# K and Q made ahead, values in three widths, and spaced reuse of two shared PSUM banks in a one-core attention kernel

## The chip, the cores and the metric

The kernel runs on one core of one Trainium2 chip. The metric is the device time of one execution in microseconds (us). The mean granted TensorE clock of each run is given too. The 21 executions of the kernel before that stood beside the experiments lie up to 1.7% to either side of their mean, so a timed experiment has four executions, with executions of the kernel before on the same chip beside it.

## The reference

```python
# x: [2048, 640] bf16, H = 32 heads of 20 columns
g = sigmoid((x * gate_w).sum(-1, keepdims=True))
q, k, v = split_heads(x @ wqkv)
a = concat_heads(softmax(q @ k.T * 20**-0.5) @ v) @ wo
h = x @ w1 + b1                     # [2048, 1536]
b = (h * tanh(softplus(h))) @ w2    # Mish
out = g * a + (1 - g) * b
```

Softmax dominates: 32 heads with 2048 x 2048 scores each. The kernel cuts them into 2048 blocks of 128 keys by 512 queries. A *group* is one chunk of 512 queries and four heads: 64 blocks, 32 groups in all, numbered 0 to 31. Groups 0 to 7 are the first query chunk.

## The kernel before

Scores come out of TensorE into PSUM, ScalarE applies the exponential to two or three blocks at a time (a *tile*, or *slot*, t), and TensorE multiplies the result by the values into `acc`. To relieve ScalarE, some pairs of blocks go to VectorE, which makes the exponential by integer arithmetic. Such a block has three terms and needs three value matmuls in place of one.

PSUM has eight banks' worth of tiles here: five for the scores of ScalarE, one for `acc`, and **two shared banks**. The shared banks take everything else: the *units* (projections K, Q, V and later the matrices of the dense branch) and the scores of the VectorE blocks. A unit alternates the banks. A VectorE score takes the bank that the next unit would take:

```python
def next_bank():
    ubank[0] ^= 1
    return banks[ubank[0]][:, :]

DPAIRS0 = (18, 34, 50)       # VectorE pairs in groups 1 to 7, block offsets
DPAIRS = (14, 30, 46, 62)    # in groups 8 to 31
LEAD = 20                    # a VectorE block is scored that many blocks ahead

def emit_D(n):
    ...
    d = banks[ubank[0] ^ 1]          # picked first ...
    scores(d[:, :], blocks[n])       # ... then K and Q are required: may run units here
    nc.vector.tensor_scalar(out=A[:, i, :], in0=d[:, :], ...)     # the eviction dA
```

Units stand in a queue, each with a slot by which it is due. `pump` gives TensorE some columns of them in each slot. If a score needs a K chunk (16 blocks) that isn't there, `require` runs the queue on the spot until it is. The slot loop is, in short:

```python
for t, ns in enumerate(tiles):
    nc.scalar.activation(E, sp.pop(t), ACT.Exp, scale=escale)   # exponential of tile t
    flush_acts()                                                # now and then: Mish
    if t in later: later.pop(t)()       # VectorE parts of a group's normalisation
    emit_S(t + 2)                       # scores two tiles ahead
    if todo and todo[0] - ns[-1] <= LEAD and gap <= 0:
        emit_D(todo.pop(0)); gap = 2
    for fn in dve_q[:2]: fn()           # VectorE exponential, two operations
    ...
    pv_quads(...)                       # value matmuls
    pump(...)                           # units, at most one (group 0: two) finished
```

A TensorE instruction that waits for a bank holds up the scores behind it: in the stretch from 64.79 us on, shown below, TensorE does nothing for 2.25 us while one unit waits for a bank. Four times, once for each query chunk, ScalarE computes Mish and makes no exponential for 8.1 us; these are the *Mish pauses*. The *tail* is what is left after the last group's exponentials.

The softmax here doesn't subtract the row's maximum and nothing guards it: scores larger than these inputs give would overflow.

## Time and profile before

| | before |
|---|---|
| median of the first 3 runs | 1058.92 us (1052.11 to 1073.89) |
| profiled run | span 1064.9 us, mean clock 0.885 |
| TensorE, ScalarE, VectorE busy | 918, 883, 652 us |
| group 0; groups 1-4; 5-7; 8-30; 31 and tail | 55.4; 137.6; 102.2; 717.9; 51.8 us |

The group times are read from the starts of the 31 copies `accS<-acc`, one at the end of each group but the last. From the page of the kernel before, busy times, then the load of TensorE and ScalarE and the granted clock in tenths, in 40 slices of the span:

```profile
PE 917.6 (86%) x6174; PEld 270.6 (25%) x6174; DVE 652.0 (61%) x1260; ACT 882.7 (83%) x750; POOL 19.8 (2%) x36
...
PE   6989888898888969998968898996998896989994
...
ACT  2979887778777899998998999989898888789771
...
PEclk8999997978689889999989999989899877799577
```

Neither TensorE nor ScalarE is full. The clock drops in places, above all in slices 7 to 15 and near the end. The clock is read with the windows view. Here are four neighbouring stretches of 3.41 us, laid on the grid of the clock records (columns: stretch, length, busy time and count of TensorE, weight load, VectorE, ScalarE, Pool; clock; DMA):

```profile
61.37:64.79 3.42, 3.42 (x32) 1.35 (x31) 1.07 (x2) 3.25 (x4) 0.00 (x0) 1.00 0.03 2
64.79:68.20 3.41, 1.16 (x9) 0.59 (x8) 2.99 (x7) 1.76 (x2) 0.00 (x0) 1.00 0.00 0
68.20:71.61 3.41, 3.41 (x22) 1.16 (x19) 2.12 (x6) 1.45 (x1) 0.00 (x0) 0.50 0.03 5
71.61:75.03 3.42, 2.51 (x13) 0.70 (x10) 1.54 (x4) 2.48 (x2) 0.52 (x1) 1.00 0.01 2
```

In the second stretch TensorE is busy for 1.16 us of 3.41; the rest is one wait for a bank. The next stretch runs at half clock: TensorE is then busy all the time, with fewer instructions (22 against 32). So a stall may be paid twice, in itself and in the half clock after it. The waits view names what makes TensorE and ScalarE wait (engine and line, what for, us in total, times, longest):

```profile
ACT E L743 <- PE Sp L565: 124.7, 153, 3.5
PE Sp L565 <- ACT E L743: 46.6, 59, 8.2
PE bank_74 L364 <- DVE dA L588: 9.6, 9, 3.1
PE bank_74 L330 <- DVE dA L588: 9.3, 9, 1.8
PE bank_74 L229 <- DVE dA L588: 8.5, 11, 1.9
PE bank_73 L565 <- DVE kT L238: 4.9, 4, 2.3
PE bank_73 L565 <- DVE hst L338: 3.9, 3, 1.9
```

`bank_73` and `bank_74` are the shared banks. L565 is a score; L229, L330 and L364 are units; L588 is the eviction (the copy out of PSUM) of a VectorE score. `kT`, `qT` and `hst` are the copies of K, Q and `h` that VectorE makes out of a shared bank. All rows of this kind together come to 69 us, 47.6 of it waits for `dA`, all but 0.9 by units. They go before the falls of the clock: of the 19 falls that follow neither the start, nor a Mish pause, nor the very end, 17 come after a piece of 3.4 us in which at least 80% of TensorE's idle time was such waits. The timeline shows how a K chunk that is not there holds up TensorE (start, length, instruction, idle time before it):

```profile
73.34 0.39 PE L229 MATMUL bank_73<-xT,wkp_104 128*128 128x512 bf16 x1
...
73.77 0.69 DVE L238 CAST kT<-bank_73 128x512 bf16<-128x512 f32 x1 [1.40 <-PE bank_73 L229]
...
74.52 0.38 PE L565 MATMUL bank_74<-qT,kT 32*128 32x512 bf16 x1 [0.79 <-DVE kT L238]
...
74.94 0.69 DVE L588 TENSOR_SCALAR dA<-bank_74 128x512 int16<-128x512 f32 x1 [0.48 <-PE bank_74 L565]
75.68 0.67 PE L271 MATMUL bank_74<-W_sb,xT 128*128 128x240 bf16 x5 [0.78 <-DVE dA L588]
```

K is finished just before the score that reads it, the score waits 0.79 us for its copy, and then the next unit, in the same bank as the score, waits 0.78 us for `dA`.

### The profile page before, as it was taken

Reading aid. Unit: us, or ns where it says so; the run is one execution under the profiler, and the core shown is the slowest. Engines: PE = TensorE matmul, PEld = TensorE weight load, DVE = VectorE, ACT = ScalarE, POOL = GpSimd, SP = SyncE. Lnnn points to the kernel's source line nnn. Section 1 sums busy time; section 2 is a strip of 40 time slices with the busy share of each in tenths; the row PEclk is TensorE's granted clock in tenths of the full one; section 3 lists DMA queues with packets and bytes.
Section 4 is the critical chain, followed back from the end, with each engine's and each line's share of the span. In section 5 each row is a group of like instructions: output and inputs, shape, how many; then the busy total and the mean of one; then the engine's idle time right before and its main releaser. Section 6 shows DMA issues by size and latency. Waiting matters only on the chain.

```text
span 1064.9 us, 15307 instructions
## 1 busy us (share of the span) xinstructions
PE 917.6 (86%) x6174; PEld 270.6 (25%) x6174; DVE 652.0 (61%) x1260; ACT 882.7 (83%) x750; POOL 19.8 (2%) x36
## 2 busy tenths in 40 slices
PE   6989888898888969998968898996998896989994
PEld 3433332222122212222212222221232221222221
DVE  2366555545466747776765777766577664577556
ACT  2979887778777899998998999989898888789771
POOL 5000000000000000000000000000000000000000
PEclk8999997978689889999989999989899877799577
DMA  7000000000400000000000000000000000000000
GB/s 226 5 2 1 2 1 1 2 1 1 149 1 2 2 1 1 8 8 14 2 1 2 1 8 14 7 1 2 2 1 2 2 1 1 14 13 1 1 2 25
DMA packets 22215, 14.16 MB, mean 13 GB/s; under 512 B 15968, under 2 KB 20192, under 8 KB 22144
## 3 DMA queue, kind: packets, MB, share of 16 engines
q1 hardware_dynamic: 20512, 12.16, 3.8%
q0 software_dynamic: 320, 0.82, 0.4%
q8 instruction: 48, 0.79, 0.3%
q10 hardware_dynamic: 1312, 0.20, 0.1%
q14 instruction: 23, 0.19, 0.1%
HBM read 10.04 MB, written 2.62 MB: 12 GB/s over the span
## 4 chain that ended last, share of the span: by engine, by line
PE 51%; DVE 21%; ACT 18%; issue 4%; DMA 3%; SPq 2%; DVEq 0%; ACTq 0%
ACT E L743 15%; PE Sp L565 14%; PE acc L637 14%; DVE dA L588 5%; PE bank_74 L364 3%; PE bank_73 L364 3%; PE bank_73 L229 3%; PE bank_74 L229 3%; PE bank_74 L330 2%; PE bank_73 L330 2%; DVE dm L614 2%; PE bank_73 L565 2%; DVE dm L607 2%; ACT hst L352 1%; PE bank_74 L565 1%
## 5 line engine op out<-in xcount | busy, mean ns | idle before, releaser
L743 ACT ACTIVATE E<-Sp 128x1536 bf16<-128x1536 f32 x726 | 847.4, 1245 | 143.5 <-PE Sp L565 124.7
L565 PE MATMUL Sp<-qT,kT 32*128 32x512 bf16 x1814 | 316.5, 416 | 52.4 <-ACT E L743 46.6
L637 PE MATMUL acc<-E,VA 128*32 128x512 bf16 x1814 | 218.7, 426 | 4.9 <-DVE accS L654 4.6
L588 DVE TENSOR_SCALAR dA<-bank_73 128x512 int16<-128x512 f32 x118 | 81.2, 688 | 140.7 <-PE bank_73 L565 129.9
L565 PEld LDWEIGHTS <-kT 32*128 32x128 bf16 x2048 | 82.7, 92 | 294.3 <-issue 263.5
L588 DVE TENSOR_SCALAR dA<-bank_74 128x512 int16<-128x512 f32 x116 | 79.4, 684 | 93.5 <-PE bank_74 L565 89.1
L637 PEld LDWEIGHTS <-VA 128*32 128x32 bf16 x2516 | 70.3, 97 | 190.9 <-issue 178.2
L614 DVE TENSOR_TENSOR dm<-dm 128x1024 f16<-128x1024 f16 x117 | 80.6, 689 | 2.6
L616 DVE TENSOR_TENSOR dB<-dA,dm 128x1024 bf16<-128x1024 bf16 x117 | 79.7, 681 | 0.0
L565 PE MATMUL bank_73<-qT,kT 32*128 32x512 bf16 x118 | 49.4, 419 | 10.4 <-DVE kT L238 4.9
L565 PE MATMUL bank_74<-qT,kT 32*128 32x512 bf16 x116 | 47.4, 409 | 9.5 <-DVE kT L238 3.6
L330 PE MATMUL bank_74<-xT,w_sb 128*128 128x512 bf16 x125 | 45.8, 419 | 9.3 <-DVE dA L588 9.3
L611 DVE TENSOR_SCALAR dm<-dm 128x1024 f16<-128x1024 bf16 x117 | 50.2, 429 | 4.0
L607 DVE TENSOR_SCALAR dm<-dA 128x1024 int16<-128x1024 int16 x117 | 50.0, 427 | 4.0
L637 PE MATMUL acc<-dN,VA 128*32 128x512 bf16 x234 | 51.5, 437 | 0.1
L637 PE MATMUL acc<-dA,VA 128*32 128x512 bf16 x234 | 51.1, 433 | 0.0
L637 PE MATMUL acc<-dB,VA 128*32 128x512 bf16 x234 | 51.0, 433 | 0.0
L364 PE MATMUL bank_74<-w_sb,hst 128*128 128x320 bf16 x192 | 45.9, 323 | 5.9 <-DVE dA L588 4.8
L615 DVE TENSOR_SCALAR dN<-dA 128x1024 int16<-128x1024 int16 x117 | 49.5, 423 | 0.0
L364 PE MATMUL bank_73<-w_sb,hst 128*128 128x320 bf16 x192 | 44.3, 321 | 3.7 <-DVE dA L588 3.6
L364 PEld LDWEIGHTS <-hst 128*128 128x128 bf16 x384 | 26.3, 99 | 69.5 <-issue 65.7
L330 PE MATMUL bank_73<-xT,w_sb 128*128 128x512 bf16 x115 | 40.6, 403 | 2.2 <-DVE dA L588 2.2
(102 smaller groups left out, 617.2 us busy)
## 6 DMA issues: line engine op xcount, KB each, us to landing
w_sb<-in_B_w_dram SPq DMA_DIRECT2D x2, 1920.0 KB, 10.3
x_sb<-in_A_x_dram SPq DMA_DIRECT2D x4, 640.0 KB, 7.6
out_dram<-ot SPq DMA_DIRECT2D x16, 160.0 KB, 1.8
den<-accS SPq DMA_DIRECT2D x124, 2.0 KB, 1.7
rrow<-rec SPq DMA_DIRECT2D x124, 2.0 KB, 1.7
W_sb<-in_A_wqkv_dram SPq DMA_DIRECT2D x1, 1600.0 KB, 15.1
W_sb<-in_A_wqkv_dram SPq DMA_DIRECT2D x1, 800.0 KB, 8.2
wo_sb<-in_A_wo_dram POOLq DMA_DIRECT2D x4, 200.0 KB, 5.6
```

Of the source, the lines that this page charges most:

```text
L229: nc.tensor.matmul(cell["t"][:, :], lhsT=lhs(kt), rhs=xT[:, kt, c * QC : (c + 1) * QC], start=(kt == 0), stop=(kt == KT - 1),)
L330: nc.tensor.matmul(cell["t"][:, :], lhsT=lw["w1"][:, kt, ft * P : (ft + 1) * P], rhs=xT[:, kt, c * QC : (c + 1) * QC], start=(kt == 0), st ...
L364: nc.tensor.matmul(cell["t"][:, :], lhsT=lhs(k, jj), rhs=rhs(k)[:, cols], start=(k == k0), stop=(k == k1 - 1),)
L565: nc.tensor.matmul(dst, lhsT=kT[R * r : R * (r + 1), p, j * P : (j + 1) * P], rhs=qTs[c, p][R * r : R * (r + 1), :], start=True, stop=True ...
L588: nc.vector.tensor_scalar(out=A[:, i, :], in0=d[:, :], scalar1=exp_c, scalar2=0.0, op0=ALU.add, op1=ALU.max)
L607: lambda: ts(out=m, in0=A, scalar1=0x7F, scalar2=0x3F80, op0=ALU.bitwise_and, op1=ALU.bitwise_or,),
L611: lambda: ts(out=t, in0=mf, scalar1=exp_k, scalar2=exp_k * EXP_M, op0=ALU.mult, op1=ALU.add),
L614: lambda: tt(out=t, in0=t, in1=t, op=ALU.mult),
L615: lambda: ts(out=N, in0=A, scalar1=0x7F80, scalar2=None, op0=ALU.bitwise_and),
L616: lambda: (tt(out=B, in0=Ab, in1=t, op=ALU.mult), done_()),
L637: nc.tensor.matmul(acc[R * r : R * (r + 1), :], lhsT=VA[:, j, p, (DH + 1) * r : (DH + 1) * r + R], rhs=es[r][k], start=(j == 0 and k == 0) ...
L743: nc.scalar.activation(E[:, 0:nw, :], sp.pop(t)[:, 0:nw, :], ACT.Exp, scale=escale)
```

## The change

It has three parts. K and Q of a group become due 20 blocks and four slots before their first block, so that a VectorE score finds them (part *ahead*). The value projections are made in widths of one, two and four head groups in place of three and four, spread over four groups, and the VectorE pairs of the first chunk move: two pairs instead of three in groups 1 to 4, four in groups 5 to 7 (part *values*, which includes the *pairs*). A unit may not start in a bank that took a VectorE score in this slot or was closed less than two slots ago, and a VectorE score avoids such a bank unless it is getting late (part *spacing*).

```diff
-    DPAIRS0 = (18, 34, 50)
+    DPAIRS0 = (30, 54)
...
+    bank_free = [0, 0]
+    now = [0]
...
-    dve_of_group = [() if g == 0 else DPAIRS0 if g < NP else DPAIRS for g in range(len(groups))]
+    dve_of_group = [() if g == 0 else DPAIRS0 if g < 5 else DPAIRS for g in range(len(groups))]
... (one_step, when a unit is finished)
             cur[1] = None
+            bank_free[ubank[0]] = now[0] + 2
... (ready, asked before a unit starts)
+        if now[0] and bank_free[ubank[0] ^ 1] > now[0]:
+            return False
...
-        add(("q", c, p), lambda: q_unit(p, c), slot(c, p, 0) - 5, front)
+        add(("q", c, p), lambda: q_unit(p, c), ahead((c * NP + p) * 64), front)
...
+    def ahead(n):
+        return tile_at[max(0, n - LEAD)] - 4
...
-            add(("k", p, c), lambda p=p, c=c: k_unit(p, c), slot(0, p, 4 * c) - 5)
+            add(("k", p, c), lambda p=p, c=c: k_unit(p, c), ahead(64 * p + 16 * c))
...
-                add_v(c * NJ, 2, 1, 3)
-                add_v(c * NJ + 2, 2, 1, 3)
-        if p in (2, 3):
-            for j in range(8 * (p - 2), 8 * (p - 1)):
-                add_v(j, 1, 4, 4, True)
+                add_v(c * NJ, NJ, 1, 1)
+            elif p == 2:
+                add_v(c * NJ, 2, 2, 2)
+                add_v(c * NJ + 2, 2, 2, 2)
+            elif p in (3, 4):
+                for j in range(8 * (p - 3) + 2 * c, 8 * (p - 3) + 2 * c + 2):
+                    add_v(j, 1, 4, 4, True)
... (emit_D)
         d = banks[ubank[0] ^ 1]
+        bank_free[ubank[0] ^ 1] = now[0] + 1
... (slot loop)
-        if todo and todo[0] - ns[-1] <= LEAD and gap <= 0:
+        now[0] = t if t >= slot(0, 1, 0) else 0
+        lead = todo[0] - ns[-1] if todo else 10 * LEAD
+        if lead <= LEAD and gap <= 0 and (bank_free[ubank[0] ^ 1] <= t or lead < LEAD - 6):
```

## The prediction

> **What bounds it.** By the page ScalarE is busy 883 us of 1064.9, TensorE 918, VectorE 652. The exponentials alone (groups view, 726 activations) are 847 us; a 3-block one takes 1.45 us and a 2-block one 1.02, so a 64-block group with 4 VectorE pairs needs about 27.7 us of ScalarE. Copies of acc mark the groups: groups 1 to 7 take 36, 32, 34, 36, 32, 36, 34 us; the best later stretch (400 to 540 us, clock 1.00) takes 26 to 30 each. Against that bound I count about 40 us lost in groups 1 to 7 and about 55 in groups 8 to 31 (the four Mish pauses of about 8 us apart).
>
> **Where it goes.** The waits show TensorE held by the two shared banks: about 47 us of first unit matmuls waiting for the eviction dA, and 20 us of VectorE-block scores waiting for kT, qT or hst in the same bank. The second cost is larger: the granted clock is 0.5 or 1, in pieces of 3.4 us, and it falls just after a piece in which TensorE was busy under about 65%. Nearly every fall outside Mish and tail follows such a bank wait (after 67, 207, 223, 243, 260, 310, 341, 702, 845 us and others). About 175 us run at half clock that way. The Trainium skill, "TensorE: Matmul & The Clock Gate", Part 1, gives two clock states and a free-running window of about 3.4 us; the trace agrees, but here no fully idle window is needed for a fall.
>
> **What the change does.**
> - Before, a VectorE block at offset 34 or 50 is scored 20 blocks ahead, when its K chunk is not yet due, so K is forced in line, in the very bank already picked for the score. After, they are due before that. The waits for kT and qT in groups 1 to 8 (about 11 us direct, plus the half-clock pieces) should go.
> - A unit no longer starts in the slot of a VectorE score (one slot is about 1.23 us, the eviction 0.69), and a score avoids a bank closed under two slots ago. I expect 60 to 70% of the dA waits gone. What stays: VectorE working in order behind the normalisation's DMA (rec and rrow waits, 22 us).
> - Pairs: 117 to 116, about +1 us of ScalarE; two instead of three in groups 1 to 4 (TensorE-bound), four instead of three in 5 to 7, where TensorE had spare time.
> - Values in three widths: 80 more short matmuls and as many weight loads (estimate 3 to 5 us of TensorE, from 0.1 us per load), spread over groups 1 to 4.
> - Units number about 140 in some 540 slots of groups 8 to 31, so the spacing does not starve them.
>
> **Sum.** Groups 1 to 7: about -23 us. Groups 8 to 31: about -24 us. Start, Mish and tail (about 20 us) unchanged; extra value work +3. About 1015 us from 1059.
>
> **What would show it.** dA waits of TensorE below 20 us in total, kT waits under 3; half clock outside Mish, start and tail below 100 us, mean clock 0.92 or more; groups 1 to 4 about 31 us, 5 to 7 about 29 to 30; ScalarE busy unchanged, its waits for Sp scores down from 125 to about 80 us.
>
> **What would make it wrong.** New falls of the clock in groups 5 to 9 because units are held back and TensorE is too idle; forced values or a drain at the start of the second chunk or at the end; VectorE lagging over a slot, so waits just move.
>
> Chances: faster by over 2% 0.79, within 2% 0.17, slower 0.04; range 983 to 1043.

## More of the kernel before

Stage by stage, from the windows view (groups 1-4, 5-7, 8-30, the rest):

```profile
55.40:193.00 137.60, 120.60 (x874) 40.99 (x872) 79.40 (x172) 109.60 (x95) 2.35 (x4) 0.93 0.01 2
193.00:295.20 102.20, 87.11 (x496) 21.63 (x496) 52.61 (x97) 81.40 (x71) 1.00 (x1) 0.79 0.12 40
295.20:1013.10 717.90, 628.99 (x4218) 175.28 (x4217) 470.25 (x883) 632.93 (x536) 0.00 (x0) 0.90 0.02 4
1013.10:1064.90 51.80, 35.36 (x214) 10.86 (x213) 31.62 (x65) 24.02 (x21) 0.00 (x0) 0.73 0.04 14
```

ScalarE is busy for 80% of the first two stages and 88% of the third.

## The result, and the profile after

The changed kernel takes 997.7 us in the median (989.22 to 1000.07, four runs), the kernel before 1062.47 us (1052.11 to 1073.89, four runs). The ratio is 0.9407, with a 95% interval of 0.9304 to 0.9509. This ratio, and every one below, is the mean time of one kernel's fast runs over that of the other's of the same rounds, so it is not quite the ratio of the medians. It is faster, inside the predicted range.

The same lines of the page for the changed kernel:

```profile
PE 874.1 (88%) x6181; PEld 270.5 (27%) x6250; DVE 647.8 (65%) x1269; ACT 876.3 (88%) x751; POOL 19.0 (2%) x36
...
PE   5999998888898688999979998997998969889894
...
ACT  3899999899898989999988999989999997996881
...
PEclk7999999998699789999967999996999996995877
```

ScalarE's load rises from 83 to 88%, with as much work as before. TensorE's busy time falls by 44 us. The part of it that lies in half clock falls from 213 to 159 us; since the 128x512 matmuls of a unit start about 410 ns apart at half clock and 226 ns at full, I estimate that about 27 of the 44 us come from that. Part of the rest is not real: 6181 matmuls stand against 6250 weight loads, so 69 matmul records are missing. The waits that answer to those shown of before (L576 is the score, L231, L332 and L366 are the units, L600 is `dA`):

```profile
ACT E L755 <- PE Sp L576: 65.3, 85, 4.4
PE Sp L576 <- ACT E L755: 52.3, 77, 8.0
PE bank_74 L366 <- DVE dA L600: 1.8, 4, 0.8
PE bank_74 L332 <- DVE dA L600: 3.7, 4, 2.2
PE bank_74 L231 <- DVE dA L600: 0.8, 1, 0.8
PE bank_73 L576 <- DVE kT L240: 1.6, 1, 1.6
PE bank_74 L576 <- DVE hst L340: 6.4, 5, 1.7
```

The `dA` rows of both banks sum to 12.3 us (47.6 before), the `kT` rows to 1.6 (8.5 before). ScalarE waits 65 us for scores instead of 125. Two kinds did not shrink: scores that wait for `hst` (5.7 us before, 6.4 now) and for `qT` (2.9 and 3.0). The stages:

```profile
56.20:172.80 116.60, 109.63 (x899) 41.53 (x913) 68.43 (x160) 112.14 (x100) 2.08 (x4) 1.00 0.01 2
172.80:258.60 85.80, 73.87 (x493) 20.25 (x501) 59.13 (x112) 77.28 (x67) 0.52 (x1) 0.87 0.15 47
258.60:945.40 686.80, 611.96 (x4180) 176.82 (x4218) 470.76 (x884) 627.76 (x536) 0.00 (x0) 0.90 0.02 4
945.40:995.70 50.30, 33.85 (x214) 10.64 (x214) 31.57 (x65) 25.11 (x22) 0.00 (x0) 0.75 0.04 14
```

Groups 1 to 4 gained 21 us, groups 5 to 7 gained 16, groups 8 to 30 gained 31, the rest nothing to speak of. In the first two stages the clock rose from 0.93 to 1.00 and from 0.79 to 0.87. In the third it did not rise. The bank waits fell in the three stages by 13, 7 and 21 us (14.0 to 0.8, 9.8 to 3.0, 43.5 to 22.0), so in the third the direct waits that went come to about two thirds of the gain. (The profiled run of before is 4 us above its kernel's median.)

Two theories have to be told apart from several rivals. **Theory A**: bank waits and the clock falls that they set off are the loss, and spacing removes most of it. **B**: K and Q ahead is what counts. **C**: the balance of TensorE work in the first chunk is what counts. About the clock: **A** says that half clock costs time of its own, **D** says that it only marks time in which TensorE has nothing to do.

### The profile page after: what moved, and what is told of

Its sections match the earlier page's. It is cut to its first block, busy times and chain, and to the rows that moved or that the text cites. A ratio compares the mean times of both kernels' runs of the same rounds, so it can differ in the third digit from the quotient of the medians.

```text
span 995.7 us, 15399 instructions
## 1 busy us (share of the span) xinstructions
PE 874.1 (88%) x6181; PEld 270.5 (27%) x6250; DVE 647.8 (65%) x1269; ACT 876.3 (88%) x751; POOL 19.0 (2%) x36
## 4 chain that ended last, share of the span: by engine, by line
PE 45%; ACT 29%; DVE 14%; issue 7%; DMA 3%; SPq 2%; DVEq 0%; ACTq 0%; another core or an unknown queue 0%
ACT E L755 26%; PE Sp L576 13%; PE acc L649 13%; PE bank_74 L366 3%; PE bank_73 L366 3%; DVE dA L600 3%; PE bank_73 L231 2%; PE bank_74 L231 2%; ACT hst L354 2%; PE bank_74 L332 2%; PE bank_74 L576 1%; PE bank_73 L332 1%; DVE dm L626 1%; DVE rrow L685 1%; DMA rrow<-rec 1%
## 5 line engine op out<-in xcount | busy, mean ns | idle before, releaser
L576 PE MATMUL Sp<-qT,kT 32*128 32x512 bf16 x1816 | 310.7, 408 | 61.8 <-ACT E L755 52.3
L649 PE MATMUL acc<-E,VA 128*32 128x512 bf16 x1816 | 214.0, 416 | 6.3 <-DVE accS L666 6.0
L576 PEld LDWEIGHTS <-kT 32*128 32x128 bf16 x2048 | 82.4, 92 | 270.1 <-issue 250.0
L600 DVE TENSOR_SCALAR dA<-bank_73 128x512 int16<-128x512 f32 x116 | 79.7, 687 | 104.6 <-PE bank_73 L576 101.0
L600 DVE TENSOR_SCALAR dA<-bank_74 128x512 int16<-128x512 f32 x116 | 79.1, 682 | 72.2 <-PE bank_74 L576 71.7
L576 PE MATMUL bank_74<-qT,kT 32*128 32x512 bf16 x116 | 46.2, 398 | 13.0 <-DVE hst L340 6.4
L576 PE MATMUL bank_73<-qT,kT 32*128 32x512 bf16 x116 | 47.9, 413 | 1.6 <-DVE kT L240 1.6
L366 PE MATMUL bank_74<-w_sb,hst 128*128 128x320 bf16 x204 | 47.6, 325 | 1.0 <-DVE dA L600 0.6
L366 PEld LDWEIGHTS <-hst 128*128 128x128 bf16 x384 | 28.4, 99 | 61.0 <-issue 56.5
L366 PE MATMUL bank_73<-w_sb,hst 128*128 128x320 bf16 x180 | 41.0, 324 | 1.9 <-DVE dA L600 1.7
L332 PE MATMUL bank_74<-xT,w_sb 128*128 128x512 bf16 x115 | 38.6, 391 | 4.1 <-DVE dA L600 3.7
L666 DVE COPY accS<-acc 128x512 f32<-128x512 f32 x31 | 21.4, 690 | 24.6 <-PE acc L649 24.6
```

The source lines that it names most:

```text
L332: nc.tensor.matmul(cell["t"][:, :], lhsT=lw["w1"][:, kt, ft * P : (ft + 1) * P], rhs=xT[:, kt, c * QC : (c + 1) * QC], start=(kt == 0), st ...
L366: nc.tensor.matmul(cell["t"][:, :], lhsT=lhs(k, jj), rhs=rhs(k)[:, cols], start=(k == k0), stop=(k == k1 - 1),)
L576: nc.tensor.matmul(dst, lhsT=kT[R * r : R * (r + 1), p, j * P : (j + 1) * P], rhs=qTs[c, p][R * r : R * (r + 1), :], start=True, stop=True ...
L600: nc.vector.tensor_scalar(out=A[:, i, :], in0=d[:, :], scalar1=exp_c, scalar2=0.0, op0=ALU.add, op1=ALU.max)
L649: nc.tensor.matmul(acc[R * r : R * (r + 1), :], lhsT=VA[:, j, p, (DH + 1) * r : (DH + 1) * r + R], rhs=es[r][k], start=(j == 0 and k == 0) ...
```

## The experiments

All twelve kernels gave the correct result. Four were run on one chip at a time, with the kernel before on the same chip. The medians of before were there 1061.62, 1066.02 and 1067.82 us. "Half clock" is 2 x (1 - mean clock) x span, for the records know only full and half. "Bank waits" are the times, in one profiled run, that TensorE sat idle before an instruction that writes a shared bank until VectorE or ScalarE released it.

| kernel | median us | ratio to before (95%) | groups 1-4 / 5-7 / 8-30 us | bank waits; of these dA, kT | mean half clock us |
|---|---|---|---|---|---|
| before | 1062.47 | 1 | 138 / 102 / 718 | 69; 47.6, 8.5 | 256 (21 runs) |
| changed | 997.70 | 0.941 (0.930-0.951) | 117 / 86 / 687 | 27; 12.3, 1.6 | 183 |
| only_space | 1023.83 | 0.962 (0.951-0.973) | 138 / 107 / 677 | 36; 10.9, 10.1 | 209 |
| only_ahead | 1048.08 | 0.990 (0.979-1.001) | 129 / 92 / 711 | 62; 51.5, 0.8 | 228 |
| only_values | 1033.44 | 0.975 (0.964-0.986) | 135 / 92 / 699 | 51; 41.8, 1.8 | 201 |
| only_pairs | 1026.42 | 0.961 (0.954-0.967) | 125 / 94 / 701 | 47; 38.8, 0.8 | 182 |
| only_widths | 1074.57 | 1.004 (0.995-1.013) | 140 / 106 / 713 | 71; 48.3, 10.2 | 271 |
| no_space | 1017.01 | 0.964 (0.954-0.975) | 120 / 86 / 708 | 46; 39.2, 0.3 | 178 |
| no_ahead | 1000.87 | 0.932 (0.922-0.942) | 128 / 81 / 688 | 27; 11.4, 1.6 | 174 |
| no_values | 1005.04 | 0.940 (0.930-0.949) | 120 / 90 / 671 | 32; 11.7, 3.2 | 178 |
| mish_warm | 994.07 | 0.931 (0.923-0.939) | 117 / 86 / 687 | 30; 14.2, 1.6 | 154 |
| floor_warm | 981.66 | 0.923 (0.917-0.929) | 119 / 83 / 673 | 28; 13.0, 2.1 | 96 |
| floor_sham | 989.85 | 0.929 (0.921-0.936) | 118 / 88 / 673 | 29; 13.1, 2.1 | 160 |
| floor_late | 990.80 | 0.928 (0.921-0.936) | 126 / 83 / 674 | 19; 12.1, 1.6 | 116 |

Ratios come from fast runs: two of the four for only_space and no_ahead, three for only_ahead, only_values, no_values and only_widths, all four for the others. The half clock column is the mean of all runs, slow ones too (the 16 fast runs of before alone give 246). The group and wait columns come from one profiled run each. Of the profiled runs those of the kernel before, only_space and no_ahead were slow, which here means a lower clock in that run, so their group times are compared with care.

### One part alone, and one part left out

**only_space** is the kernel before plus `bank_free`, `now`, the test in `ready` and the condition on `emit_D`.

> The kernel before plus the spacing of the two banks alone. Theory A (the bank waits and the clock falls they set off are the loss, and spacing removes them): groups 8 to 30 fall from 718 to about 687 us as in the changed kernel, groups 1 to 7 by about 10 of the 37 us; 1015 to 1025 us, dA waits of TensorE under 15 us. Rival B (K and Q ahead is what counts, spacing only shifts waits): 1045 us or more, groups 8 to 30 above 705.

The ratio is 0.962, the median 1023.83 us, inside A's range. `dA` waits fall from 47.6 to 10.9 us, and groups 8 to 30 take 677 us. A holds there. In groups 1 to 7, where A had expected 10 us, spacing alone gained nothing: `kT` waits stayed at 10.1 us and those groups take 138 and 107 us.

**only_ahead** is the kernel before with the two due times alone.

```diff
-            add(("k", p, c), ..., slot(0, p, 4 * c) - 5)
+            add(("k", p, c), ..., ahead(64 * p + 16 * c))
-        add(("q", c, p), ..., slot(c, p, 0) - 5, front)
+        add(("q", c, p), ..., ahead((c * NP + p) * 64), front)
```

> The kernel before plus K and Q due ahead alone. Theory A: kT waits fall from 8.5 to under 3 us, groups 8 to 30 stay at 710 to 720, groups 1 to 7 gain 10 to 15 us: 1045 to 1050 us. Rival B: 1025 us or less.

As A expected: 1048.08 us, `kT` waits 0.8 us, groups 8 to 30 nearly as before. The interval of the ratio (0.979 to 1.001) reaches 1, so that this part alone makes the kernel faster is not certain. Group 0 pays for it: 58.9 us instead of 55.4 in the profiled run, as one more K chunk is due in it. B falls.

**only_values** is the kernel before with the widths and the pairs.

> The kernel before plus the three value widths and the moved VectorE pairs alone. Theory A: groups 8 to 30 unchanged, groups 1 to 4 gain about 8 us, groups 5 to 7 nothing, as K is still forced in line there: 1050 to 1058 us. Rival C (balance of TensorE work over groups 1 to 7 is the main gain): 1030 us or less.

It gave 0.975 and 1033.44 us, more than A allowed and not quite what C asked for. In my prediction this part cost 3 us. So the part was split further down.

**no_space** is the changed kernel without the test in `ready` and with the old condition on `emit_D`.

> The changed kernel without the spacing (K and Q ahead and the values kept). Theory A: groups 8 to 30 back at 705 to 720 us, dA waits back above 35 us; 1025 to 1035 us. Rival B: under 1010 us.

The median is 1017.01 us: spacing is worth about 2.4% of before on top of the other two (0.964 against 0.941, from different chips, each against before). `dA` waits are back at 39.2 us, groups 8 to 30 at 708 us. B, which wanted less than 1010, falls again; A's range of 1025 to 1035 was too high, as the other parts gave more than it knew.

**no_ahead** and **no_values** are the changed kernel with one part undone.

> The changed kernel with K and Q due as before (spacing and values kept). If the parts simply add (alone they gave ratios 0.962, 0.990, 0.975): about 0.95, 1005 to 1010 us, kT waits back at 6 us or more in groups 1 to 8. If K and Q ahead matters only while a bank is in short supply and the spacing covers it: under 1000 us, no difference from the changed kernel.

> The changed kernel with the value widths and the VectorE pairs as before. My prediction's view (values cost 3 us and give little): 1000 us or less. The view from the run of that part alone (it gave 0.975): 1012 us or more, the difference in groups 1 to 7 (about 129 + 92 us instead of 117 + 86).

Leaving out *ahead* gives 0.932 (from the two fast runs of four; its medians give 0.939), leaving out *values* gives 0.940, and the whole gives 0.941: the three can't be told apart. So the parts do not add. Once the banks are spaced, either of the other two is enough, and the second adds nothing that these runs can show. Both medians (1000.87 and 1005.04 us) fell between the two figures of their expectations. Without *ahead* the bank waits for `kT` did not come back (1.6 us, and 3.1 us before scores of ScalarE); the *pairs* keep them away, as the next runs show. Without *values*, groups 1 to 7 take 120 + 90 us, against the 129 + 92 expected.

### What the moved pairs do

```diff
# only_pairs: these two lines of the change, on the kernel before
-    DPAIRS0 = (18, 34, 50)
+    DPAIRS0 = (30, 54)
-    ... DPAIRS0 if g < NP else DPAIRS ...
+    ... DPAIRS0 if g < 5 else DPAIRS ...
# only_widths: the add_v lines of the change, on the kernel before
```

> The kernel before with the VectorE pairs of the first chunk moved alone (two in groups 1 to 4, four in 5 to 7), values as before. If the pairs made the 0.975 of values and pairs together: 1030 to 1040 us, groups 1 to 4 below 135. If they made none of it: 1055 us or more.

> The kernel before with the values in three widths alone, the pairs as before. My prediction's view (80 more short matmuls, 3 us of cost): 1060 to 1066 us. If spreading the value work is what gave the 0.975: 1030 to 1040 us.

The pairs alone give 0.961, even beyond the expectation (1026.42 us). The widths alone give 1.004, nothing (1074.57 us, above both ranges of the expectation, with before at 1067.82 on that chip). Pairs and widths together had given 0.975 on another chip, no better than the pairs alone. The waits for K, from the waits view of only_pairs and then of only_widths (the line numbers differ by the added lines):

```profile
PE bank L565 <- DVE kT L238: 0.8, 1, 0.8
```

```profile
PE bank L567 <- DVE kT L238: 10.2, 13, 2.9
```

The code explains why the waits for K went. A K chunk covers 16 blocks and was due five slots, 12.5 blocks, before its first block. A VectorE block at offset o is scored at o - 20. Offset 18 needs the chunk that starts at 16, due at 3.5, at block -2. Offset 34 needs it at 14, due at 19.5. Offset 50 needs it at 30, due at 35.5. So *every one of the three old offsets* needed its K chunk before it was due, and K was made in line whenever the queue was not ahead of its dues. The new offsets lie late in their chunks: 30 needs K at 10 (due 3.5), 14, 46 and 62 need it 6.5 blocks after it is due, and 54 needs it at 34, 1.5 blocks before. So moving the pairs takes the waits for K away by itself, as *ahead* does, without the load on group 0. It also takes one pair of three, with its extra value matmuls, out of groups 1 to 4, where TensorE had most to do. No run tests the two apart. only_ahead, which leaves the pairs where they were, takes 129 + 92 us in groups 1 to 7, and only_pairs 125 + 94.

Not all of its 0.961 is explained. In the profiled runs groups 8 to 30 take 701 us with the moved pairs and 718 without, although their code is the same. The only difference that I can name is that ScalarE has 472 instead of 470 blocks before group 8, so the tiles of three and of two blocks fall differently on the groups. With spacing the sign is the other way round: 677 and 671 us with 470 blocks (only_space, no_values), 687 and 688 with 472 (changed, no_ahead); but floor_sham, further down, has 472 too and takes 673. These are single profiled runs with different clock falls in them, and no run tests this. It stays open.

### Does half clock cost time of its own?

There is evidence before any experiment. From the clock records and the TensorE matmuls of all fourteen traces I counted, for each piece of 3.4 us at full clock (after the first 25 us, to the end), how busy TensorE was in it and whether the next piece ran at half clock:

```
TensorE busy in the piece   pieces   next at half clock
under 50%                       99                   98
50 to 60%                       83                   59
60 to 70%                      153                   69
70 to 80%                      250                   12
80% and more                  2766                    0
```

And the 21 executions of the *same* kernel before, in which nothing differs but chance and chip, have spans from 1047.0 us (mean clock 0.907) to 1082.7 us (0.861). A line through them has a slope of 0.29 us of span for each us at half clock, with a correlation of 0.97. The 16 fast runs alone give a slope of 0.28, so it does not rest on slow runs. The four runs of each of the other kernels give slopes from 0.25 to 0.43. This is a correlation. Three runs try to make the clock the cause.

**floor_warm** adds 177 useless matmuls to the changed kernel, in slots with little TensorE work:

```diff
+    def dummies(n):
+        d = banks[ubank[0] ^ 1]
+        for _ in range(n):
+            nc.tensor.matmul(d[:, :], lhsT=xT[:, 0, 0:P], rhs=xT[:, 0, 0:QC], start=True, stop=True)
...
-            credit -= pump(min(credit, max(room, 300.0)), 1)
+            done_cols = pump(min(credit, max(room, 300.0)), 1)
+            credit -= done_cols
+            light = 1500 - (used - 800) - done_cols
+            if light > 0 and bank_free[ubank[0] ^ 1] <= t:
+                dummies(min(2, -(-light // 512)))
```

> The changed kernel plus 177 useless 512-column matmuls (38 us of TensorE at full clock), at most two in a slot that carries little TensorE work. Theory A: fewer pieces under 65% busy, half clock outside start, Mish and tail (about 78 us) falls below 40, time falls by 5 to 15 us although work was added. Rival D: the added work costs time or nothing: 998 to 1015 us.

Useless work made the kernel faster: 981.66 us, ratio 0.923 with an interval (0.917 to 0.929) that lies wholly below that of the changed kernel (0.930 to 0.951). Mean half clock falls from 183 to 96 us; in the profiled run 17 us of it lie outside start, Mish and tail, where A had asked for less than 40. Bank waits did not fall (28 us against 27). The clock line of its page, to be held against that of the changed kernel above:

```profile
PEclk7999999999999789999999999999799998999996
```

**floor_sham** has the same matmuls at the same places with 8 columns instead of 512 (`d[:, 0:8]`, `rhs=xT[:, 0, 0:8]`): the same order of instructions, little activity.

> The same 177 extra matmuls at the same places as in the run with useless matmuls in light slots, but 8 columns instead of 512: the same order, hardly any activity. Theory A (those matmuls helped by keeping the clock up): half clock back to 150 to 200 us, time 993 to 1002 us as for the changed kernel. Rival E (they helped by shifting order and times): 980 to 986 us again.

```profile
PEclk7999999899699799999979999997899995999977
```

Half clock is back at 160 us (146 to 174 in its four runs, against 90 to 106 in floor_warm's), and the time is 989.85 us. All four times (987.25 to 999.10) lie above all four of floor_warm (980.90 to 985.93), on two chips whose runs of before have medians within 0.2%. But the ratio intervals (0.921 to 0.936, and 0.917 to 0.929) overlap, and it came out below the 993 to 1002 that A expected. So: the large matmuls keep the clock up, and the small ones do not, which is shown; that about 8 us of the gain comes through the clock is likely from the runs and not beyond doubt; the remaining difference between floor_sham and the changed kernel is within the noise. The slope of 0.29 would give (160 - 96) x 0.29 = 19 us, from which the cost of 177 large matmuls has to come off; floor_warm shows about half of it.

**mish_warm** puts 24 useless matmuls into each of the four Mish pauses of the changed kernel, before the scores of the slot after Mish (`if hot[0] == t: dummies(24)`).

> The changed kernel plus 24 useless 512-column matmuls (about 5 us) into the next free bank in each of the four Mish pauses, so that TensorE is not idle there. Theory A (half clock costs time of its own): the half-clock pieces after Mish, about 78 us in the changed kernel, fall below 25 us, and the time falls by 10 to 25 us, to 973 to 988 us. Rival D (half clock is a mere mark of idle time; ScalarE's Mish sets the pace there anyway): no change, 995 to 1002 us.

The clock around the four pauses of the changed kernel, and then of this one (windows view). The stretches are not of one length, and the second and fourth of the changed kernel begin near the fall, 8 and 6 us after the start of the pause, so not their mean clocks are to be compared but the time at half clock, which is twice the length x (1 - clock):

```profile
326.00:345.00 19.00, 11.17 (x72) 2.91 (x72) 7.84 (x15) 17.86 (x14) 0.00 (x0) 0.73 0.00 1
507.00:536.00 29.00, 27.55 (x131) 5.96 (x133) 14.18 (x27) 20.68 (x18) 0.00 (x0) 0.54 0.01 1
681.00:700.00 19.00, 13.97 (x77) 3.92 (x76) 6.88 (x13) 16.45 (x14) 0.00 (x0) 0.56 0.00 0
817.00:843.00 26.00, 21.98 (x103) 4.57 (x103) 8.65 (x17) 19.48 (x17) 0.00 (x0) 0.54 0.01 1
```

```profile
326.00:345.00 19.00, 16.41 (x110) 5.96 (x109) 9.14 (x17) 18.96 (x16) 0.00 (x0) 1.00 0.00 1
505.00:540.00 35.00, 32.78 (x222) 10.66 (x221) 20.77 (x40) 33.45 (x29) 0.00 (x0) 0.95 0.01 1
680.00:700.00 20.00, 17.85 (x109) 6.01 (x108) 9.01 (x17) 19.41 (x16) 0.00 (x0) 0.91 0.00 1
815.00:855.00 40.00, 37.17 (x188) 9.32 (x184) 17.50 (x33) 31.62 (x26) 0.00 (x0) 0.66 0.02 5
```

Half clock in these stretches falls from 10, 27, 17 and 24 us to 0, 3.5, 3.6 and 27: the first fall went, the second and third shrank to about one piece, the fourth stayed. The sum is 34 us where A had asked for less than 25. And new pieces at half clock came elsewhere, and the total fell only from 183 to 154 us in the mean. The median of 994.07 us misses A's expectation of 973 to 988 and lies in the noise of the changed kernel (ratio intervals 0.923 to 0.939 and 0.930 to 0.951). Filling the large pauses is not enough: in the profiled run of the changed kernel more of the half clock follows ordinary slots than Mish (89 us against 79 by where it begins, 109 against 58 by what TensorE had waited for; see the section on the prediction).

### What the waits that remain cost

In the changed kernel scores still wait for `hst` and `qT`. The timeline shows VectorE at work, in order, with the two last parts of a normalisation (L685, L687) and the VectorE exponential ahead of the copy that frees the bank:

```profile
643.71 0.39 PE L332 MATMUL bank_74<-xT,w_sb 128*128 128x512 bf16 x1
...
644.16 0.72 DVE L685 STREAM_SHUFFLE rrow<-rrow 128x512 f32<-128x512 f32 x1
...
644.92 0.69 DVE L687 TENSOR_TENSOR oT<-accS,rrow 128x512 bf16<-128x512 f32 x1
...
646.47 0.74 DVE L340 TENSOR_SCALAR hst<-bank_74,b1f 128x512 f32<-128x512 f32 x1
...
647.27 0.37 PE L576 MATMUL bank_74<-qT,kT 32*128 32x512 bf16 x1 [1.66 <-DVE hst L340]
```

The unit's last matmul ends at 644.10 us, and the copy `hst` at 647.21, 3.1 us later; a slot takes 1.37 us in the mean (995.7 us over 727 exponentials).

**floor_late** is floor_warm with one more slot of spacing when VectorE has such a part in that slot.

```diff
-            bank_free[ubank[0]] = now[0] + 2
+            bank_free[ubank[0]] = now[0] + 2 + (heavy[0] == now[0] or now[0] + 1 in later)
...
-        bank_free[ubank[0] ^ 1] = now[0] + 1
+        bank_free[ubank[0] ^ 1] = now[0] + 1 + (heavy[0] == now[0])
```

> The kernel with useless matmuls in light slots, and the spacing of a bank one slot longer when VectorE has a part of a normalisation in that slot (1.4 us of shuffle and product ahead of the eviction). If the waits that remain come from VectorE working in order behind those parts: waits of block scores for hst, qT and the like fall from 11 to under 5 us, time 972 to 980 us. If not: waits unchanged, 980 to 986 us.

The waits fell as expected: all bank waits from 28 to 19 us, those of VectorE scores for `hst` and `qT` from 8.4 to 0.3 us. The time did not: 990.80 us against 981.66, and half clock rose from 96 to 116 us. Groups 1 to 4 take 126 us instead of 119 in the profiled runs. So taking these waits away in this manner does not pay. What the price is, the run can't say, for two things changed in it: the filler asks the same `bank_free` as the units, so that the longer spacing also stopped some of it. The trace has 163 weight loads of useless matmuls where floor_warm has 177. Fewer fillers may be why half clock rose; that the units then come in bunches, with light slots between, is another guess. Neither is tested.

## Why the prediction was right or wrong

The time was predicted as 1015 us with a range of 983 to 1043, 60 us wide, and measured as 997.7. The direction and the main mechanism held. The sum was too small by about 17 us, mostly in groups 1 to 7.

- **"TensorE held by the two shared banks": right.** Bank waits fell from 69 to 27 us, and each run with spacing shows `dA` waits of 11 to 14 us, each without it 39 to 52.
- **"I expect 60 to 70% of the dA waits gone": right in kind**, a little more went, 74% (47.6 to 12.3 us).
- **"The waits for kT and qT ... should go", by K and Q due ahead: half right.** The waits for K went (8.5 to 1.6 us). Those for `qT` did not (2.9 to 3.0 us), and none of them had been in groups 1 to 8: in the trace of before they lie in groups 19, 25 and 27. And I gave the gain to *ahead* alone; the moved pairs do it too (`kT` waits 0.8 us in either run alone), and without *ahead* the changed kernel is as fast.
- **"Pairs: 117 to 116, about +1 us of ScalarE": the step that failed.** I costed the move by what it adds to ScalarE and by where TensorE had time to spare, and did not ask at which block each offset needs its K chunk. All three old offsets needed K before its due slot; of the new ones only 54 does, by 1.5 blocks. Alone the move is worth 4% (1026.42 us against a before of 1067.82 on that chip). Not all of that is explained, as told above. In the changed kernel it matters less: without the moved pairs and the widths (no_values) groups 1 to 7 still gain 30 us in the profiled runs, against 37.5 with them, and the whole is not told apart. So how much of the missing 17 us comes from this step stays open.
- **"80 more short matmuls ... estimate 3 to 5 us": not shown either way.** The widths alone gave 1.004 with an interval of 0.995 to 1.013. What they are good for I can only see in group 0: 58.9 and 58.4 us in the profiled runs with *ahead* but the old widths, 55.6 and 56.2 with both.
- **"Groups 1 to 7: about -23 us": too small**, they lost 37.5 us (239.8 to 202.3). **"Groups 8 to 31: about -24 us":** 32.6 us (769.7 to 737.1). Both terms err to the same side.
- **"Half clock outside Mish, start and tail below 100 us": met or missed by how one counts.** By where it begins, it fell from 174 us to 89. But 17 of the 79 us counted as Mish begin at 680.7 us, after a piece in which TensorE's one long idle time was a wait of 1.33 us for `hst`, over before the pause began (679.86). Counted by what TensorE waited for in the piece before, it fell from 184 to 109 us. **"Mean clock 0.92 or more": wrong**, 0.902 profiled, 0.908 in the mean. The pieces after the Mish pauses grew, from 48 to 79 us by the first count and from 38 to 58 by the second; I had taken them as constant.
- **"A score avoids a bank closed under two slots ago":** the change does that, but the waits of scores for `hst` did not fall (5.7 to 6.4 us). In the case shown above VectorE finished more than two slots behind. This was in the prediction as "VectorE working in order behind the normalisation's DMA".
- **"ScalarE's waits down from 125 to about 80 us":** 65 us.
- **How much the clock contributes.** Half clock fell from 246 us (16 fast runs of before) to 183 (4 fast runs), and at 0.28 us each that is 18 us of the 65 between the medians. Bank waits in the profiled runs fell by 42 us. The two sum to 60 us. This is an account and no proof, for a bank wait need not lie on the critical path.

The Trainium skill, "TensorE: Matmul & The Clock Gate", section "A second HAM failure mode: psum-queue depth-cycling", describes just this kind of loss: short idle times between groups of matmuls that cycle through PSUM banks make the clock alternate between two states. This agrees, with 174 us at half clock in the kernel before that follow neither Mish nor start nor tail. The same page, under "Architectural detail", says that VectorE is a strict FIFO; the timeline above agrees: the copy `hst` comes after L685 and L687, and the score that needs its bank waits 1.66 us.

## What to carry to other kernels

When two users share a PSUM bank, don't hand it on in the same slot: leave the engine that empties it one slot, and let the next user start later rather than wait in an in-order queue. When work is scored or loaded ahead, check each offset against the time at which its inputs are *due*, for an input made in line holds up what stands behind it (0.79 and then 0.78 us in the first timeline above), and shifting the offset may be cheaper than moving the input. And look at the clock next to each stall: a stretch of 3.4 us in which TensorE was busy under 50% was followed by half clock in 98 of 99 cases here, one of 50 to 60% in 59 of 83, and cheap filler matmuls in light slots took another 2% off (floor_warm is faster than both kernels; about half of that also came with the tiny matmuls of floor_sham, within the noise).

## What the Trainium skill lacked or had wrong

- "TensorE: Matmul & The Clock Gate", Part 1, lets the clock fall "after ≥1 idle window (~3.4µs)", and the page's table of goals advises to avoid idle gaps over about 3 us. The section on depth-cycling, cited above, has short idle times be enough, but gives no share of busy time at which it happens. In these traces no idle window is needed: the clock fell after 98 of 99 pieces in which TensorE was busy under 50%, after 128 of 236 between 50 and 70%, and after none of 2766 at 80% or more. The longest gap in the piece before a fall was under 2.3 us in 199 of the 238 cases and 1.4 us in the median. The two clock states and the length of the piece, 3.4 us, agree with the page.
- The same page, under "Terms", puts the penalty of a throttled clock at the throttled time x (1 - K/N), which is 0.5 us for each us at half clock. In this kernel, where ScalarE shares the load, the 21 runs of before show 0.29 us of span for each us (a correlation, from 0.854 to 0.907 of mean clock).
- The page's table of goals advises warm-up matmuls for benchmarks. It doesn't say that useless matmuls in light slots of a running kernel can pay: 177 of them (512 columns) took the ratio to before from 0.941 to 0.923, and the same number with 8 columns left the clock low (160 us at half clock against 96), at a ratio of 0.929; the intervals of the two overlap.
